# A one-core decode block: head-by-head query projection, a bf16 bias product, and 64 streamed columns in the wo and w1 products

## The chip, the cores and the metric

The kernel runs on one core of a Trainium2 chip. The metric is the device time of one execution in microseconds (us). One execution is also recorded by the hardware profiler; its span, from the first to the last instruction, is about 1.5 us shorter than the time in most runs. Engines are named as in the profile: PE (matrix products), PEld (its weight loads), DVE (vector), ACT (scalar), POOL, and SP, whose sequencer (SPq) issues most transfers.

## The reference, cut to what matters

```python
# x: 4 x 1 x 640 (batch 4, one token); 32 heads of 128; cache of 4096 positions; all bf16
q = (layernorm(x) @ wq)                                   # wq 640 x 4096
scores = einsum("bhqd,bhkd->bhqk", q, k_cache) * 128**-0.5 # k_cache 4 x 32 x 4096 x 128
o = einsum("bhqk,bhkd->bhqd", softmax(scores), v_cache)
h = x + o.reshape(4, 1, 4096) @ wo                        # wo 4096 x 640
g = layernorm(h) @ w1 + b1                                # w1 640 x 1728
out = h + (g * tanh(log(1 + exp(g)))) @ w2                # w2 1728 x 640
```

The two caches are 268 MB, the weights 15 MB. There is one token for each of 4 batch rows, so all the projections are products with 4 columns.

## The kernel before, where the change touches it

The heads go in four groups of 8; a tile is the K or V cache of one batch row and one head group (8.39 MB). K tiles are multiplied by the broadcast query on DVE, folded on PE, and V is multiplied on PE. SP asks for tiles as their buffers come free; a V tile can't replace wq before the query has been made. The start:

```python
# query projection: wq is (128, 5, 4096) in a cache buffer, lnT the normalised x, transposed
for h in range(2):
    for c in range(DC):                       # DC = 5 chunks of the 640 inputs
        for hg in range(NHG):                 # 4 head groups, one per 32 output partitions
            mm(red[hg*32:(hg+1)*32, h, :], lnT[:, c, :], wq[:, c, o:o+512], ...)
# two copies red -> q_all (bf16); then spread each head's query over its partitions
for hg in range(NHG):
    for b in range(N):
        for g in range(G):                    # 4 * 4 * 8 = 128 products, 32 rows, 128 columns
            mm(red[:, (2+hg) % 4, b*128:(b+1)*128], sel[r, b, ...], q_all[r, g*128:(g+1)*128], ...)
```

The tail, after the last cache tile (the `mark` and `need` calls, which are semaphores, are left out):

```python
def wo_mm(k):                                 # head group k: 8 x 5 = 40 products of 4 columns
    for j in range(G):
        for c in range(DC):
            w = wo_sb[:, k, j, :].rearrange("p (m c) -> p c m", c=DC)[:, c, :]   # every 5th column
            mm(y_ps[:, c, :], w, a_t[:, k, j, :], False, done)
# ... o, softmax sums, wo_mm(0..3); y -> DVE -> mean and variance by two fp32 products ...
for c0, c1 in ((0, 2), (2, 4), (4, 5)):       # w1 arrives in three pieces
    if c1 == DC - 1:                          # with the second: bias * std, in fp32
        mm(red[:, 2, 0:56], ident_f[:, :], b1s[...], False, False)
    for j in [FM] + list(range(FM)):          # FM = 13: 14 blocks of outputs
        for c in range(c0, c1):
            w = w1_sb[:, c, 0:FM*P].rearrange("p (f j) -> p j f", j=FM)[:, j, :] # every 13th column
            mm(h1_ps[..., j, :], w, cen[:, c, :], False, done)                  # 4 columns
# then h onto the output's bank (40 small products), the activation on DVE and ACT,
# 56 products with w2 (160 columns, 4 side by side in 32-column strips), copy, store
```

The softmax here doesn't subtract the row's maximum and nothing guards it: scores larger than these inputs give would overflow.

## Time and profile before

The time is 663.18 us (median of 3 runs, 662.7 to 663.21). What matters of the profile, whose span is 661.1 us:

| what | us |
|---|---|
| wq landed / first K tile landed | 15.9 / 36.1 |
| one cache tile, landing to landing | 19.3 |
| last piece of w2 landed | 657.5 |
| end | 661.1 |

Landings are read from the transfer records of the trace, piece by piece. The page's slices come first. The rows are 40 equal slices of the span; PEclk is the granted clock of PE in tenths, DMA the busy share of the transfer engines in tenths.

```profile
...
PEclk9768787968658697958767887888876879797965
DMA  9999999999999999999999999999999999999997
GB/s 390 437 444 440 441 417 420 441 436 442 433 436 416 444 436 432 436 440 420 436 436 436 436 436 440 416 444 433 432 440 436 420 440 432 432 440 440 408 420 293
...
```

The transfer engines are at 9 tenths in every slice but the last. They moved 283.50 MB at a mean 429 GB/s, and from 1.65 us to about 655 the records of transfers show never fewer than 16 in flight. So the bytes and their rate set the time of this kernel; at this rate it can gain only before the first transfer or after the last. The next lines are the timeline of the start (start, duration, engine, line, operation, count, and in brackets the idle time before it and what ended it).

```profile
...
16.02 4.42 PE L708 MATMUL red<-slotC,lnT 128*32 128x512 bf16 x40 [6.80 <-PEq L49]
...
21.22 10.31 PE L708 MATMUL red<-q_all,sel 32*128 32x128 bf16 x128 [0.78 <-PEq L49]
...
31.56 0.33 SPq L250 DMA_DIRECT2D slotC<-in_A_v_cache_dram  x1
31.57 0.59 ACT L375 CAST q_bc<-red 128x512 bf16<-128x512 f32 x1 [2.38 <-PE red L708]
...
36.20 8.76 DVE L515 TENSOR_TENSOR slotA<-slotA,q_bc 128x8192 bf16<-128x8192 bf16 x2 [27.27 <-DMA slotA<-in_A_k_cache_dram]
...
```

Read the last line first: DVE was idle 27.27 us and was released by the landing of the K tile, not by the query, whose last copy to q_bc ends at 32.2. The 128 selecting products are the 10.31 us in the second line.

The chain of waits at the end (start, duration, what):

```profile
...
624.24 22.11 DMA slotB<-in_A_wo_dram
...
646.49 1.75 PE y_ps L708 x40
...
648.49 0.63 PE misc L708 x2
...
649.59 5.33 PE red L708 x72
...
656.76 2.16 PE red L708 x31
...
```

From the landing of a piece of wo at 646.35 on, PE and DVE (and once ACT) work in turn, and the chain shows no wait for a transfer: 40 wo products, 72 records on the w1 bank, the activation, the w2 products. Last, the stretches of 3.41 us in which the clock is granted; the columns after the length are the busy times (and counts) of PE, PEld, DVE, ACT and POOL, then the granted clock, the DMA share and GB/s.

```profile
...
core 0: us, PE busy (x) PEld busy (x) DVE busy (x) ACT busy (x) POOL busy (x), PEclk, DMA share, GB/s
641.49:644.90 3.41, 3.03 (x64) 2.73 (x62) 1.51 (x3) 0.00 (x0) 0.00 (x0) 0.50 0.99 416
644.90:648.31 3.41, 2.78 (x67) 2.63 (x64) 0.05 (x1) 0.00 (x0) 0.00 (x0) 0.50 1.02 425
648.31:651.72 3.41, 3.17 (x34) 3.04 (x34) 1.50 (x11) 1.58 (x2) 0.00 (x0) 0.50 1.01 416
651.72:655.13 3.41, 3.41 (x66) 3.24 (x65) 0.19 (x1) 0.00 (x0) 0.00 (x0) 0.50 1.00 416
655.13:658.54 3.41, 2.31 (x88) 1.99 (x78) 1.35 (x6) 0.25 (x1) 0.00 (x0) 0.50 0.33 123
...
```

PE is busy for 82 to 100% of the first four stretches and still has clock 0.50 throughout.

### The profile page before, as it was taken

The page shows a single profiled execution, that of the slowest core. Times are in us where ns is not written, and L with a number is a line of the kernel's source. Part 1 is how long each engine was busy: PE and PEld are TensorE (multiplying, and loading weights), DVE is VectorE, ACT ScalarE, POOL GpSimd, SP SyncE. Part 2 cuts the span into 40 slices and gives each one's busy share as a digit, 9 for nine tenths or more (in the row PEclk, how much of TensorE's full clock was granted, in tenths as well). Part 3 has the DMA queues.
Part 4 walks back from the last instruction along what each step waited for, and adds up shares of the span by engine and source line. Part 5 has one row for each costly group of instructions (what it writes and reads, how often), then busy time and mean ns, then how long its engine had stood idle before and what let it go on. Part 6 is the DMA issues. An engine that isn't in the chain of part 4 may idle for free. (4 is left out here: it accounts for less than half of the span.)

```text
span 661.1 us, 5195 instructions
## 1 busy us (share of the span) xinstructions
PE 396.9 (60%) x2747; PEld 80.8 (12%) x1787; DVE 406.9 (62%) x252; ACT 41.6 (6%) x158; POOL 2.6 (0%) x14
## 2 busy tenths in 40 slices
PE   0856658568317595738407485838434656765767
PEld 0600000101101010101100010000110001010246
DVE  1077988386048779757218798849306798848612
ACT  0200000000000000000000000000000000000011
POOL 1000000000000000000000000000000000000000
PEclk9768787968658697958767887888876879797965
DMA  9999999999999999999999999999999999999997
GB/s 390 437 444 440 441 417 420 441 436 442 433 436 416 444 436 432 436 440 420 436 436 436 436 436 440 416 444 433 432 440 436 420 440 432 432 440 440 408 420 293
DMA packets 6978, 283.50 MB, mean 429 GB/s; under 512 B 1012, under 2 KB 1208, under 8 KB 2232
## 3 DMA queue, kind: packets, MB, share of 16 engines
q1 hardware_dynamic: 6640, 283.27, 99.2%
q8 instruction: 7, 0.11, 0.1%
q10 hardware_dynamic: 328, 0.09, 0.1%
q14 instruction: 3, 0.02, 0.0%
HBM read 283.35 MB, written 0.01 MB: 429 GB/s over the span
## 5 line engine op out<-in xcount | busy, mean ns | idle before, releaser
L515 DVE TENSOR_TENSOR slotA<-slotA,q_bc 128x8192 bf16<-128x8192 bf16 x32 | 140.6, 4416 | 104.3 <-DMA slotA<-in_A_k_cache_dram 104.3
L515 DVE TENSOR_TENSOR slotB<-slotB,q_bc 128x8192 bf16<-128x8192 bf16 x32 | 140.7, 4418 | 16.7 <-DMA slotB<-in_A_k_cache_dram 16.7
L526 DVE TENSOR_REDUCE s_f<-red 128x64 f32<-128x1024 f32 x64 | 78.0, 1219 | 97.7 <-PE red L718 97.6
L718 PE MATMUL red<-slotA,ident 128*128 128x512 bf16 x480 | 136.4, 447 | 0.0
L718 PE MATMUL red<-slotB,ident 128*128 128x512 bf16 x480 | 127.1, 424 | 0.0
L708 PE MATMUL red<-slotA,ident 128*128 128x512 bf16 x32 | 14.6, 456 | 118.9 <-PEq L49 118.9
L708 PE MATMUL pv<-slotC,e 128*32 128x512 bf16 x768 | 53.4, 439 | 36.9 <-PEq L49 33.9
L708 PE MATMUL red<-slotB,ident 128*128 128x512 bf16 x32 | 14.1, 440 | 87.5 <-PEq L49 87.5
L394 ACT ACTIVATE ex<-s_f 128x64 bf16<-128x64 f32 x64 | 16.4, 256 | 503.1 <-DVE s_f L526 503.1
L540 DVE TENSOR_TENSOR e<-ex,hmask 128x512 bf16<-128x512 bf16 x64 | 39.8, 684 | 0.0
L708 PEld LDWEIGHTS pv<-slotC,e 128*32 128x32 bf16 x768 | 22.7, 108 | 96.2 <-issue 82.9
L708 PEld LDWEIGHTS red<-slotA,ident 128*128 128x128 bf16 x32 | 3.2, 99 | 187.7 <-issue 187.6
L708 PEld LDWEIGHTS red<-slotB,ident 128*128 128x128 bf16 x32 | 3.1, 98 | 170.6 <-issue 170.6
L708 PEld LDWEIGHTS o_ps<-pv_sb,selo 128*32 128x32 f32 x136 | 13.5, 109 | 63.0 <-issue 62.9
L708 PE MATMUL o_ps<-pv_sb,selo 128*32 128x128 f32 x136 | 18.0, 276 | 0.0
L708 PE MATMUL pv<-slotA,e 128*32 128x512 bf16 x256 | 14.6, 380 | 0.4 <-PEq L49 0.4
L404 ACT COPY pv_sb<-pv 128x512 f32<-128x512 f32 x16 | 9.4, 586 | 70.4 <-PE pv L708 70.4
L394 ACT ACTIVATION_READ_ACCUMULATOR ex<-s_f 128x1 f32 x64 | 11.9, 186 | 0.0
L708 PE MATMUL red<-q_all,sel 32*128 32x128 bf16 x128 | 10.3, 273 | 0.8 <-PEq L49 0.8
L708 PEld LDWEIGHTS red<-q_all,sel 32*128 32x128 bf16 x128 | 10.1, 124 | 1.6 <-issue 1.6
L708 PEld LDWEIGHTS pv<-slotA,e 128*32 128x32 bf16 x256 | 7.0, 97 | 23.4 <-issue 17.7
L565 DVE RECIPROCAL rl<-misc 32x1 f32<-32x1 f32 x4 | 0.6, 151 | 14.3 <-PE misc L708 14.3
(96 smaller groups left out, 77.8 us busy)
## 6 DMA issues: line engine op xcount, KB each, us to landing
slotC<-in_A_v_cache_dram SPq DMA_DIRECT2D x2, 4096.0 KB, 40.6
slotC<-in_A_wq_dram SPq DMA_DIRECT2D x1, 5120.0 KB, 15.9
slotB<-in_A_wo_dram SPq DMA_DIRECT2D x3, 1280.0 KB, 17.7
slotB<-in_B_w_dram SPq DMA_DIRECT2D x2, 864.0 KB, 25.0
slotB<-in_A_wo_dram SPq DMA_DIRECT2D x1, 960.0 KB, 22.1
slotA<-in_B_w_dram SPq DMA_DIRECT2D x1, 960.0 KB, 25.2
slotA<-in_B_w_dram SPq DMA_DIRECT2D x1, 640.0 KB, 22.4
slotB<-in_B_w_dram SPq DMA_DIRECT2D x1, 432.0 KB, 26.4
```

What stands on the lines that cost most here:

```text
L394: lambda: a.activation(out=ex[:, sl], in_=s_f[:, sl], func=ACT.Exp, scale=SCALE, accum_out=rs[:, b, s : s + 1],),
L404: lambda: a.copy(out=pv_sb[:, :, :].rearrange("p r d -> p (r d)"), in_=pv[:, :]),
L515: lambda: v.tensor_tensor(out=t, in0=t, in1=q_bc[:, hg, b, :].unsqueeze(1).to_broadcast([P, RS, Dh]), op=ALU.mult,),
L526: lambda: v.tensor_reduce(out=s_f[:, s * RS : (s + 1) * RS], in_=red[:, k : k + 2, :].rearrange("p k (r c) -> p (k r) c", c=CW), axis=AX.X ...
L540: lambda: v.tensor_tensor(out=e[:, sl, :], in0=ex[:, sl].unsqueeze(2).to_broadcast([P, RS, G]), in1=hmask[:, :].unsqueeze(1).to_broadcast( ...
L565: dv.do(lambda: v.reciprocal(out=rl[:, :], in_=l_ps), ("rl", hg), DV)
L708: lambda: nc.tensor.matmul(out_, lhsT=lhsT, rhs=rhs, start=start, stop=stop, skip_group_check=skip),
L718: return t.add_instruction(mybir.InstMatmult(name=nc.get_next_instruction_name(), engine=mybir.EngineType.PE, ins=[t.lower_ap(rhs), t.lowe ...
```

## The change

Three parts, meant to shorten the start and the tail. (1) The projection writes each head's query to its own 4 partitions (lnT is padded so that a shifted slice puts the 4 rows in place), so 4 selecting products of 128 rows and 512 columns replace 128 small ones. (2) The bias product, fp32 before, becomes a high and a low bf16 part, moved ahead of the last w1 piece. (3) The moving operand of the wo and w1 products is the 4 columns repeated 16 times: 64 columns stream, of which 4 are used. The wide products are meant to bring PE's clock up: in the stretches above the 4-column products kept PE busy for 82 to 100% and the clock was 0.50.

```diff
-        for h in range(2):
+        GK = G // CG
+        for r in range(GK):
             for c in range(DC):
-                for hg in range(NHG):
+                for k in range(CG):
+                    g = k * GK + r
                     mm(
-                        red[hg * QD : (hg + 1) * QD, h, :], lnT[:, c, :], wq[:, c, o : o + 512],
+                        red[k * QD : (k + 1) * QD, 0, :], lnT[:, c, QD - N * (g + 1) : 2 * QD - N * (g + 1)],
+                        wq[:, c, :].rearrange("p (h g d) -> p g h d", g=G, d=Dh)[:, g, :, :],
 ... (cut)
+        for b in range(N):
+            mm(
+                red[:, (1 + b) % 4, :], sel[:, b * G : (b + 1) * G, :].rearrange("p g q -> p (g q)"),
+                q_all[:, :], True, True, ("qb", b),
+            )
 ... (cut: wo)
-                    mm(y_ps[:, c, :], w, a_t[:, k, j, :], False, done, "y" if done else None)
+                    mm(
+                        y_w[:, c, :, :], w, a_t[:, k, j, :].unsqueeze(1).to_broadcast([P, WD, N]),
+                        False, done, "y" if done else None,
+                    )
 ... (cut: two 512-column products with zeros open the wider bank of w1)
-            if c1 == DC - 1:
-                pe.need("b1s")
-                mm(
-                    red[:, 2, 0 : FC * N], ident_f[:, :], b1s[:, :, :].rearrange("p j n -> p (j n)"),
-                    False, False,
-                )
+            if c1 == DC:
+                pe.need("b1_lo")
+                for part in (b1_hi, b1_lo):
+                    for j0, j1 in ((0, FC // 2 + 1), (FC // 2 + 1, FC)):
+                        mm(h1_ps[:, j0:j1, :], ident[:, :], part[:, j0:j1, :], False, False)
 ... (cut: w1, as wo)
-                        h1_ps[0 : (P if j < FM else FT), j, :], w, cen[:, c, :], False, done,
+                        h1_w[0 : (P if j < FM else FT), j, :, :], w,
+                        cen[:, c, :].unsqueeze(1).to_broadcast([P, WD, N]), False, done,
```

## The prediction

> **What bounds the kernel now.** Transfers. The profile page moves 283.5 MB at a mean 429 GB/s, DMA busy tenths are 9 in 39 of 40 slices, and a count of packets in flight in the trace is 16 from 1.65 us to about 655 us. Landings come in issue order: wq at 15.9 us, the first K tile at 36.1, then a tile (8.39 MB) each 19.3 us (434 GB/s) to the end; the last w2 piece lands at 657.5. After it only 3.5 us remain. The chain of waits follows a transfer of wo landing at 646.35, then PE and DVE: wo products 1.75 us, mean 1.3, w1 products with bias 5.33 (649.59 to 654.92), activation 1.8, w2 products 2.16, copy 0.33, stores to 661.1. So only the last 15 us can respond.

> **Query projection.** The grouped timeline of the start shows 40 matmuls in 4.42 us, two copies of 0.59, then 128 selecting matmuls in 10.31 us. After: still 40 matmuls of 512 columns, one copy, 4 selecting matmuls of 512 columns (0.43 us each at the low clock, from the 128x32x512 matmuls): about 9 us off PE, q_bc ready near 24 us instead of 32.2. But the first multiply starts at 36.20 on the landing of the first K tile, and V's issue (31.56, would be about 23) only joins a queue that is full and in order. Worth 0.

> **The tail.** Windows of 3.41 us show the granted clock 1.0 or 0.5: 1.0 from 638.1 to 641.5, then 0.5 to the end, although PE is busy. [...] But a wo pair (weight load plus 4-column product) takes 43 ns at clock 1.0 (40 in 1.76 us) and 43 ns at 0.5 (40 in 1.73 us), and a w1 pair 65 to 68 ns: the weight load sets the pace, not the clock. Estimated from 128x512 products (427 ns at 0.5[...]), 64 columns need 53 or 27 ns. In w1 they hide in either state; in wo they hide at 1.0, and cost 40 x 10 ns = 0.4 us per head group at 0.5. I expect wo to stay at 1.0 and w1 to fall to 0.5 somewhere. Two 512-column zero products cost 0.4 to 0.8 us more before the third wo group, nearly hidden before the landing at 646.35.

> **Bias.** Two fp32 products (0.66 us in the w1 stream) become four bf16 ones [...] and no longer hold up the middle piece: 0.3 to 0.4 us gained on the chain. The last w1 pieces land at 651.5 and 652.55, so w1 can't end before about 654.4.

> **Limit.** w2's last piece at 657.5 allows at most 1.1 us of gain; that needs w2 at the full clock (52 products in 1.90 us would halve) or act much earlier.

> **Sum.** 0.3 to 0.4 from the bias, 0 to 0.7 from the clock in w2, minus 0 to 0.5 in wo: 663.18 to about 662.8 us. Range 661.9 to 663.9. Faster by over 2%: 0.005; within 2%: 0.985; slower: 0.01.

> **What would show it.** Landings unchanged, 19.3 us apart; first multiply still near 36.2; last query product near 23; clock 1.0 through the wo stage; wo pairs still 43 ns; w1 stage near 4.9 us; w2 landing near 657.5.

> **What would make it wrong.** Weight loads that don't overlap a 64-column product: wo and w1 pairs grow by 25 to 50 ns, costing 3 to 5 us. Or wo staying at 0.5. Or weight loads of w1 that do speed up at clock 1.0, up to the 1.1 us limit.

The trace of before has 427 ns from start to start of 128x512 products at clock 0.5 and 216 at 1.0; an eighth of these is the 53 or 27 ns for 64 columns. The four bf16 products took 0.29 us in the changed kernel (653.56 to 653.85).

## The result, and the profile after

The changed kernel takes 662.12 us (median of 4 runs, 661.6 to 662.67), the kernel before 663.01 in the same rounds. The ratio is 0.9987, with a 95% interval of 0.997 to 1.0004. A ratio here is the mean time of one kernel's fast runs over that of the other's of the same rounds, so it isn't quite the ratio of the medians. Over the nine fast runs of the two comparisons with the changed kernel the mean is 662.24 us, against 662.96 for the 13 runs of before beside them: about 0.7 us less, or 0.1%.

The page's slices of the changed kernel:

```profile
...
PEclk9768787968659796869677887888876769796867
DMA  9999999999999999999999999999999999999997
GB/s 386 444 440 444 421 409 444 437 440 434 437 424 432 436 436 436 440 432 420 440 432 440 436 440 420 436 436 429 444 440 428 424 432 436 440 440 440 400 423 299
...
```

The transfers are as they were. The timeline of its start:

```profile
...
16.12 4.17 PE L714 MATMUL red<-slotC,lnT 128*32 128x512 bf16 x40 [5.99 <-PEq L49]
...
21.07 1.02 PE L714 MATMUL red<-q_all,sel 128*128 128x512 bf16 x4 [0.78 <-PEq L49]
21.48 2.05 ACT L372 CAST q_bc<-red 128x512 bf16<-128x512 f32 x4 [0.56 <-PE red L714]
22.12 0.33 SPq L253 DMA_DIRECT2D slotC<-in_A_v_cache_dram  x1
...
35.48 8.76 DVE L512 TENSOR_TENSOR slotA<-slotA,q_bc 128x8192 bf16<-128x8192 bf16 x2 [25.89 <-DMA slotA<-in_A_k_cache_dram]
...
```

The selecting products take 1.02 us in place of 10.31, V is asked for at 22.12 in place of 31.56, and DVE still waits for the first K tile. The chain of waits at its end:

```profile
...
639.04 2.23 PE y_ps L714 x40
...
642.29 1.72 PE y_ps L714 x40
...
645.32 3.36 PE y_ps L714 x80
...
648.93 0.41 PE misc L714 x2
...
649.82 5.16 PE red L714 x74
...
656.82 2.16 PE red L714 x56
...
```

The w1 stage takes 5.16 us in place of 5.33, the two fp32 statistics products 0.41 in place of 0.63, and the w2 products 2.16 as before. The clock windows of the same stretches (this execution's own windows begin 0.4 us before the stretches chosen):

```profile
...
641.49:644.90 3.41, 3.36 (x60) 3.11 (x58) 1.75 (x4) 0.00 (x0) 0.00 (x0) 1.00 0.97 409
644.90:648.31 3.41, 3.41 (x79) 3.21 (x78) 0.04 (x1) 0.00 (x0) 0.00 (x0) 1.00 1.03 424
648.31:651.72 3.41, 2.88 (x41) 2.53 (x38) 1.81 (x13) 1.55 (x2) 0.00 (x0) 0.94 1.01 421
651.72:655.13 3.41, 3.41 (x66) 3.16 (x67) 0.13 (x1) 0.03 (x1) 0.00 (x0) 0.50 1.01 420
655.13:658.54 3.41, 2.31 (x91) 1.99 (x82) 1.41 (x6) 0.25 (x1) 0.00 (x0) 0.50 0.42 155
...
```

The clock is at 1.00 through most of wo and the first part of w1, and at 0.50 in w2. So in the profiled execution little came of it: from the last w2 landing (657.81) to the end (661.16) pass 3.35 us, against 3.59 before (657.52 to 661.11). This execution was also the slowest of the four: its span was 661.2 us, the others' 660.1 to 660.8. The experiments had to say what the others did.

### The profile page after: what moved, and what is told of

The parts are those of the page before. It is cut to its first block, busy times and chain, and to the rows that moved or that the text cites. A ratio compares the mean times of both kernels' runs of the same rounds, so it can differ in the third digit from the quotient of the medians.

```text
span 661.2 us, 4952 instructions
## 1 busy us (share of the span) xinstructions
PE 388.1 (59%) x2626; PEld 70.3 (11%) x1666; DVE 407.5 (62%) x254; ACT 40.7 (6%) x157; POOL 1.7 (0%) x12
## 5 line engine op out<-in xcount | busy, mean ns | idle before, releaser
L714 PE MATMUL red<-slotC,lnT 128*32 128x512 bf16 x40 | 4.2, 597 | 6.0 <-PEq L49 6.0
L714 PE MATMUL y_ps<-a_t,slotB 128*128 128x64 bf16 x160 | 7.6, 213 | 0.0
```

The source lines that it names most:

```text
L714: lambda: nc.tensor.matmul(out_, lhsT=lhsT, rhs=rhs, start=start, stop=stop, skip_group_check=skip),
```

## The experiments

The table gathers the last 4 us of every profile that bears on the tail. "w2 clock" is the granted clock in the w2 stage, "w2" the duration of its 56 products.

| run | w2 clock | w2, us | last w2 landing | end | difference |
|---|---|---|---|---|---|
| before | 0.5 | 2.16 | 657.52 | 661.11 | 3.59 |
| before_look | 0.5 | 2.16 | 657.72 | 661.34 | 3.62 |
| q_only | 0.5 | 2.16 | 657.54 | 661.27 | 3.73 |
| bias_only | 0.5 | 2.16 | 657.92 | 661.23 | 3.31 |
| wide_only | 1.0 | 1.27 | 657.87 | 661.08 | 3.21 |
| after | 0.5 | 2.16 | 657.81 | 661.16 | 3.35 |
| after_again | 1.0 | 1.32 | 657.55 | 660.05 | 2.50 |
| after_look | 1.0 | 1.35 | 657.54 | 660.04 | 2.50 |
| w1_wide | 0.5 | 2.17 | 657.72 | 661.98 | 4.26 |
| fill_narrow | 0.5 | 2.16 | 657.61 | 661.23 | 3.62 |
| fill | 1.0 | 1.33 | 657.84 | 660.34 | 2.50 |
| contig | 0.5 | 2.9, waits for the landing | 657.61 | 660.17 | 2.56 |

q_twice and q_late, not in the table, had clock 0.5, 2.16 us and differences of 3.66 and 3.69. So all eight profiles with 4 columns in wo and w1 had the low clock in w2, and four of the six with wide w1 products had the full one.

The difference is worth more than the time here: the landings themselves move by 0.4 us between executions, and the difference leaves that out.

### q_only: the projection alone

Edit: part (1) of the diff on the kernel before, nothing else.

> The kernel before with the query projection of the change alone. Main theory (the gain is made after the last wo landing, the projection has slack until the first K tile lands near 36 us): q_bc ready near 23.5 us in place of 32.2, first multiply still within 0.7 us of 36, ratio to before 1.000 +- 0.0007, tail from the first-part landing of the fourth wo group to the end 14.7 us as before. Rival (the projection is worth part of the gain): 0.3 to 0.9 us faster, landings of the K and V tiles earlier throughout.

Measured: 663.06 us (662.78 to 663.88, 5 runs), ratio 1.0005 (0.9992 to 1.0019). The first three cache tiles landed 0.85 us earlier (the first at 35.25 in place of 36.1), but the fourth at 94.10 (94.00 before) and the last w2 piece at 657.54 (657.52). So the projection, 9 us shorter on PE, gives nothing, as the main theory said.

### bias_only: the bf16 bias alone

Edit: part (2) on the kernel before, with 4 columns throughout.

> The kernel before with the bf16 bias product alone, 4 columns throughout. Main theory: this is where the tail's gain comes from; w1 stage about 4.95 to 5.15 us in place of 5.33 (held to that by the landing of the middle w1 piece), tail 0.2 to 0.4 us shorter, ratio 0.9995. Rival: nothing, tail 14.7 us.

Measured: 662.45 us (662.39 to 662.74), ratio 0.9993 (0.9979 to 1.0006); all five runs but one lie below the lowest of the nine runs of before beside them (662.70). In its chain of waits the w1 stage takes 4.93 us in place of 5.33:

```profile
...
650.11 4.93 PE red L717 x72
...
```

The difference falls to 3.31; the five profiles with the fp32 bias in one piece and strided 4-column products have 3.59 to 3.73. The interval doesn't exclude 1, but time, stage and difference agree: this part is worth 0.3 to 0.5 us.

### wide_only: the 64 columns alone

Edit: part (3) on the kernel before. The wide w1 products write two banks of `red` in place of one, and the fp32 bias is split in two with them.

> The kernel before with the 64-column wo and w1 products alone, bias still in fp32. Main theory (weight loads set the pace, 42 to 43 ns in wo and 59 to 60 ns in w1 in either clock state): no gain, 0 to +0.4 us, because a wo group takes 2.2 us where the clock is 0.5 and 1.7 where it is 1.0. Rival (the clock raised by the wide products makes the tail shorter): tail after the fourth wo landing 0.3 us or more shorter than 14.7 us, time 0.3 to 0.9 us lower.

Measured: 663.26 us (661.81 to 663.72), ratio 1.0001 (0.9987 to 1.0015). On the time the main theory holds, but its reason doesn't. In the profile the w1 stage took 5.91 us (the split fp32 bias cost 1.03 us for four records in place of 0.66 for two), and the clock was back at 1.0 in w2, which took 1.27 us in place of 2.16. A loss and a gain cancelled. From its chain of waits:

```profile
...
649.87 5.91 PE red L711 x74
...
657.62 1.27 PE red L711 x56
...
```

The single runs spread over 1.9 us, where those of before spread over 0.5.

### after_again and after_look: the changed kernel again

Edit: none. after_again has 5 rounds; after_look is a single look of unknown state.

> The changed kernel once more, on the chip of the three parts. Main theory: 0.2 to 0.4 us below before (ratio 0.9994 to 0.9997), about the sum of the parts; the 0.9 us of the first comparison was mostly spread of the transfers from run to run. Rival: 0.9 us below again (ratio 0.9987), interval clear of 1.

> A third profile of the changed kernel. Theory: one of two outcomes, by where the 3.41 us windows fall: w2 at clock 1.0, about 1.35 us, end 2.5 us after the last w2 landing (as in the second profile), or at 0.5, about 2.15 us, end 3.3 us after it (as in the first). Nothing between.

Measured: after_again 662.58 us (661.4 to 662.88), ratio 0.9994 (0.9981 to 1.0008), so the median gain is 0.4 us this time. But its profile, and that of after_look, show what the first profile didn't: w2 at the full clock. The chain of waits of after_look:

```profile
...
646.68 1.77 PE y_ps L714 x40
...
649.59 5.07 PE red L714 x74
...
656.50 1.35 PE red L714 x56
...
```

The w2 products take 1.35 us in place of 2.16, and the end comes 2.50 us after the last landing in place of 3.35. So the tail has two outcomes in the three profiles taken, as expected before after_look. In the clock records of after_again the clock fell to 0.5 at 651.77, one window at 0.5 full of w1 products followed, and at 655.18 it was raised again, in time for w2; after_look shows the same 0.25 us later. In the first profile it fell at 651.33 and stayed at 0.5. Its next window also held w1 products, but in it PE waited about 0.2 us for the second piece of w1 (landed at 651.70; in after_again the same wait, 651.26 to 651.50, fell before the window).

### before_look: the kernel before again

Edit: none.

> A second profile of the kernel before. Theory: in w2 the granted clock is 0.5 whatever the place of the 3.41 us windows[...]; w2 stage 2.1 to 2.2 us, end 3.5 to 3.7 us after the last w2 landing. Rival (the phase decides for both kernels): w2 at 1.0 here, end 2.5 us after that landing.

Measured: 662.85 us, clock 0.5 from 641.84 to the end, w2 2.16 us, difference 3.62. With 4 columns both profiles have the slow w2.

### w1_wide: wo back at 4 columns

Edit, on the changed kernel:

```diff
-                        y_w[:, c, :, :], w, a_t[:, k, j, :].unsqueeze(1).to_broadcast([P, WD, N]),
+                        y_ps[:, c, :], w, a_t[:, k, j, :],
```

> The changed kernel with the wo products back at 4 columns, w1 still at 64. Theory (wide wo gives nothing that the end keeps; wide w1 at the low clock [...]raises the clock for w2 in some executions): wo pairs 43 ns whatever the clock, spread of the spans as in the changed kernel (660.0 to 661.2), ratio 0.9990 to 0.9997. Rival (the wide wo products carry the gain): spans all near 661.2 and the w2 stage always near 2.1 us.

Measured: 662.9 us (661.95 to 664.59), ratio 0.9994 (0.9981 to 1.0008). The spans were 660.2 to 662.0. Two of five runs reached the short end without wide wo products, and the profiled one shows what wide wo is for. There the clock was 0.5 from 629.75 on; the two 512-column products that open the w1 bank took 0.77 us in place of 0.45 (in wide_only, at 1.0), the last two wo groups ended late, and y was copied at 649.24, 2.56 us after the fourth wo landing (646.68); before it was 1.91 (648.26 after 646.35). From its chain of waits:

```profile
...
645.28 0.77 PE red L714 x2
...
```

The window that held the end of the V products and the start of wo had a share (by the count above) of 0.66 here, from 636.58, and of 0.95 in the first profile of the changed kernel, from 637.68, and the clock rose there alone. It rose before the third wo group in all five profiles with wide wo and in five of the nine with 4 columns. So in these profiles an early rise went with wide wo products more often than with 4 columns, which neither theory had; the profiles are few, and the place of the windows differs among them.

### contig: does the weight load set the pace?

Edit, on the kernel before; results are wrong (relative error 0.044), traffic and counts the same:

```diff
-                    w = wo_sb[:, k, j, :].rearrange("p (m c) -> p c m", c=DC)[:, c, :]
+                    w = wo_sb[:, k, j, c * P : (c + 1) * P]
-                        w = w1_sb[:, c, 0 : FM * P].rearrange("p (f j) -> p j f", j=FM)[:, j, :]
+                        w = w1_sb[:, c, j * P : (j + 1) * P]
```

> The kernel before, with the wo and w1 weights of each product taken as 128 adjacent columns in place of every 5th (wo) and every 13th (w1); results wrong on purpose, traffic the same. If the strided weight load sets the pace of a pair: wo pairs fall below 40 ns and w1 pairs well below 59 ns at the same clock, the w1 stage is then held by the landing of its last piece (near 652.5) and ends before 654.2, and the w2 stage either starts before 656 and ends within 0.5 us of the last w2 landing; gain 0.5 to 1.1 us and no more. If the pace is a floor per pair or the clock: pairs unchanged, no gain.

Measured: 661.8 us (661.68 to 662.02), ratio 0.9984 (0.997 to 0.9997). Its timeline, all at clock 0.5:

```profile
...
646.69 1.20 PE L708 MATMUL y_ps<-a_t,slotB 128*128 128x4 bf16 x40 [1.06 <-DMA slotB<-in_A_wo_dram]
...
649.53 1.02 PE L708 MATMUL red<-cen,slotB 128*64 128x4 bf16 x28 [0.33 <-DMA slotB<-in_B_w_dram]
...
655.12 0.30 PE L708 MATMUL red<-w_tail,act 64*4 64x160 bf16 x4 [1.10 <-DVE act L697]
...
655.35 2.61 PE L708 MATMUL red<-slotA,act 128*4 128x160 bf16 x52
...
658.01 0.33 DVE L704 CAST o_bf<-red 128x160 bf16<-128x160 f32 x1 [2.94 <-PE red L708]
...
```

The 40 wo products take 1.20 us, where columns 10 bytes apart took 1.73 in the kernel before; their starts are 27 ns apart in place of 40. The first 28 w1 products take 1.02 us in place of 1.92, with starts 27 ns apart in place of 59 to 60. The clock and the columns are the same, so the stride of the weight load set the pace. The activation was ready at 655.12 in place of 656.76, 1.64 us earlier, but the end came only 0.94 us earlier in these two profiles (1.1 in the medians): the w2 stage, still at the low clock, now waits for its last piece (657.61) and ends 0.4 us after it. That is the limit that the prediction named.

### fill and fill_narrow: holding the clock up

Edit of fill, on the changed kernel: 96 columns in w1, and four products of 512 columns without use where PE waits.

```diff
+        fill(pv)            # an identity product with 512 columns of q_bc into a bank that is free
         pe.need("st")
+        fill(y_full)
         pe.need("cen")
-                        cen[:, c, :].unsqueeze(1).to_broadcast([P, WD, N]), False, done,
+                        cen[:, c, :].unsqueeze(1).to_broadcast([P, 24, N]), False, done,
+        fill(y_full)
+        fill(y_full)
         pe.need("act")
```

The wider w1 bank takes all four banks of `red`, so y2 moved to another. fill_narrow has the same four products on bias_only, with 4 columns everywhere.

> The changed kernel with 96 columns in the w1 products and four 512-column products without use put where PE waits (before the copy of y, before the centred rows, two before the activation). Theory (the w2 products' clock is what varies between executions of the changed kernel: 2.16 us cold, 1.35 us at full clock): the clock stays 1.0 to the end in every execution, w2 stage about 1.3 us, end within 0.5 us of the last w2 landing, spans of all runs 659.9 to 660.4, ratio to before about 0.9985. If the products without use delay the chain or the clock falls anyway: no better than the changed kernel, spans 660 to 661.3.

> The kernel before with the bf16 bias and the four products without use, wo and w1 at 4 columns. If the wide columns are what keeps the clock up: clock 0.5 in w1 and w2, w2 stage about 2.15 us, the products without use take 0.43 us each and delay the chain by 0 to 0.4 us, ratio 0.9990 to 1.0003. If the four products alone are enough: w2 about 1.35 us and 661.8 us, as with the wide columns.

Measured: fill is correct and takes 661.85 us (661.66 to 661.97), ratio 0.9983 (0.9969 to 0.9996), with spans of 660.1 to 660.4; in its trace the clock is 1.0 from 639.16 to 659.64. Four of its windows, and the w2 stage from its timeline:

```profile
...
644.90:648.31 3.41, 3.35 (x78) 3.15 (x77) 0.00 (x0) 0.00 (x0) 0.00 (x0) 1.00 1.04 426
648.31:651.72 3.41, 3.10 (x43) 2.59 (x41) 1.81 (x13) 1.52 (x2) 0.00 (x0) 1.00 1.02 424
651.72:655.13 3.41, 3.41 (x78) 3.16 (x79) 0.12 (x1) 0.06 (x1) 0.00 (x0) 1.00 1.00 410
655.13:658.54 3.41, 2.06 (x94) 1.33 (x80) 1.74 (x7) 0.25 (x1) 0.00 (x0) 1.00 0.37 138
...
```

```profile
...
656.82 0.24 PE L715 MATMUL o_ps<-w_tail,act 64*4 64x160 bf16 x4 [0.77 <-DVE act L704]
...
656.99 1.13 PE L715 MATMUL o_ps<-slotA,act 128*4 128x160 bf16 x52
658.17 0.33 DVE L711 CAST o_bf<-o_ps 128x160 bf16<-128x160 f32 x1 [1.40 <-PE o_ps L715]
...
```

PEclk is 1.00 where the kernel before has 0.50, and 52 of the w2 products take 1.13 us in place of 1.90. All five runs are short, so the spread of the changed kernel goes when the clock is held. fill_narrow takes 662.84 us (662.66 to 662.91), ratio 0.9996 (0.998 to 1.0013): clock 0.5 from 629.55 to the end, w2 2.16 us. Four products without use are not enough: its clock was low before the first of them, and no window of its tail had a share above 0.69. With the wide columns (64 in wo and 96 in w1) the clock rose, and no window counted less than 0.46 until the one in which w2 ended. Whether the wider columns or the four products would do alone was not run.

fill is the fastest correct kernel, by 1.1 us over the kernel before. Its last copy starts 0.33 us after the last w2 landing (657.84, 658.17), so little more is to be had from PE's clock.

### q_twice and q_late: how much slack has the start?

Edit, on the kernel before: all 128 selecting products twice (q_twice), or 64 of them twice (q_late).

```diff
-        for hg in range(NHG):
+        for rep, hg in [(r, h) for r in range(2) for h in range(NHG)]:          # q_twice
+        for rep, hg in [(0, 0), (0, 1)] + [(1, h) for h in range(NHG)]:         # q_late
```

> The kernel before with the 128 selecting products of the query projection done twice, about 10 us more on PE ahead of the first multiply. Main theory (the full in-order transfer queue makes the start worth nothing): first multiply moves from 36.2 to about 42.5 us, the landings of all later tiles and the end don't move, ratio 1.000 +- 0.001. Rival (the start is on the path of the time): 6 to 10 us slower (ratio 1.010 to 1.015).

> The kernel before with 64 of the 128 selecting products done twice, about 5 us more on PE at the start (the doubling of all of them moved the first multiply from 36.2 to 43.7 us and cost 2.3 us at the last K and V landings, with one tile asked for only 2.8 us before its predecessor landed). Theory (the start is free until an issue comes within a few us of the queue running dry): first multiply near 37.5 to 39 us, the fifth issue near 65 us and still 8 us or more ahead of the landing before it, landings 19.3 us apart throughout, ratio 1.000 +- 0.001. Rival (every us of the start beyond the first K tile's landing costs a third of a us): ratio 1.001 or more, last K and V landings 0.5 us later.

Measured: q_twice takes 666.0 us (665.01 to 667.69, 4 runs), ratio 1.0054 (1.0039 to 1.007). Both theories are wrong. The first multiply and the issues of the next tiles, from its timeline:

```profile
...
43.73 8.76 DVE L515 TENSOR_TENSOR slotA<-slotA,q_bc 128x8192 bf16<-128x8192 bf16 x2 [34.64 <-ACT q_bc L375]
...
```

```profile
...
71.42 0.33 SPq L250 DMA_DIRECT2D slotA<-in_A_k_cache_dram  x1
92.47 0.33 SPq L250 DMA_DIRECT2D slotC<-in_A_v_cache_dram  x1
...
```

The multiply starts 7.5 us later, and so do the buffers come free. The V tile was asked for at 92.47, only 2.8 us before the landing ahead of it (95.25); in the kernel before the same issue was 10.3 us ahead (83.67, 94.0). In the records of transfers in flight the engines lost 0.9 us between 90 and 100 us, where the kernel before lost none. The landing of the next K tile is 2.4 us late (135.01, 132.6 before), and from there on the tiles keep their 19.3 us to the end. Counted in bytes moved, this execution falls behind the kernel before by 1.5 us between 92 and 97 us: 0.9 of idle engines, and the rest in transfer records that took longer (2.70 us in the mean in place of 2.42). The issue at 71.42, 3.8 us ahead of its landing, cost 0.2, and one at 130.15, 4.9 us ahead, nothing. Another 0.6 us was lost between 34 and 42 us, when no tile was late; why stays open. The profile is that of the fastest of the four runs (665.01), so the others lost more. q_late moved the first multiply to 38.0; the issue at 85.74 was 8.3 us ahead of the landing before it (94.08), and the closest of the whole run, at 590.85, 5.8 us. It lost nothing: 663.05 us, ratio 1.000 (0.9983 to 1.0017). So the start has slack of at least 1.8 us and less than 7.5. The projection moves the query forward from 32.2 us to 23.5, where the K tile's landing at 35 to 36 already covers it.

## Why the prediction was right

**Time.** 662.8 was predicted, with 661.9 to 663.9 as range; the first comparison gave 662.12, the second 662.58. The range of 2 us holds both outcomes of w2, and no change at all as well, so the total tests little; the terms of the sum are what the experiments tested. Three of the first comparison's four spans are 660.8 or less, and two of the second's five; the kernel is the same, so that the first came out lower may be chance.

**Transfers bound the body.** Right. Tiles land 19.3 us apart in both kernels, and fill, contig and the changed kernel all end between 660.0 and 661.2 us in their profiles.

**Projection worth 0.** Right, shown by q_only. The reasoning behind it, that a full queue makes the start free, is true only as far as q_late: q_twice shows that the slack ends before 7.5 us.

**Bias 0.3 to 0.4 us.** Right: 0.5 us in the medians of bias_only, 0.3 to 0.4 in the difference, 0.40 in the w1 stage. The w1 stage was expected near 4.9 us. It took 4.93 in bias_only, and 5.07 (after_look) and 5.16 (first profile) in the changed kernel: its 64 columns lengthen the last 14 products (1.19 us in after_look, 1.09 in bias_only), and in the first profile PE waited for the second piece.

**Weight loads, not the clock, set the pace of wo and w1.** Right, shown by contig, and by the spacing of the records: w1 products start 59 to 60 ns apart at clock 0.5 with 4 columns and at both clocks with 64. A group of wide wo products takes 2.23 us at 0.5 (for its first 2.05 us) and 1.72 at 1.0, 0.5 us more where 0.4 was expected. "Clock 1.0 through the wo stage" was half right: in the first profile the first group ran at 0.5, because the clock rose at 641.09 there.

**0 to 0.7 us from the clock in w2.** That w2 can get the full clock was right, the size a little low: the limit of 0.7 for this term was too small by 0.1. w2 at the full clock takes 0.81 to 0.84 us less (2.16 to 1.35 or 1.32), and this happened in two of three profiles. The prediction's middle (0.4 us of gain in all) gave it too little weight; the mean gain of nine runs is 0.7.

**At most 1.1 us.** Right. contig and fill, two quite different ways to shorten the tail, both stop there: ratios 0.9984 and 0.9983, and 2.56 and 2.50 us after the last landing.

Where did 9 us of PE work and a doubled clock go? The 9 us lay under the wait for the first K tile. In wo and w1 the clock isn't the pace: 4-column wo products start 40 ns apart at either clock (before), and 64-column w1 products 59 to 60 (after). What is left is 0.3 us of bias and 0.8 us of w2 in the executions in which w2 runs at clock 1.0 (two of three profiles).

## What to carry to other kernels

Ask what a product's pace is before paying for clock. Here, with 4 columns, the weight load was the pace, and its stride mattered where the clock didn't: it took the starts of w1 products from 27 to 59 ns apart at clock 0.5 (contig, before), and at clock 1.0 the 59 stayed as they were (after). Columns streamed for nothing gave w2, the stage that did need it, the full clock in four of the six profiles with wide w1 products (1.27 to 1.35 us in place of 2.16), and in none of the eight with 4 columns. By the count, no window at 0.5 with a share below 0.72 was followed by 1.0, and the share depended on where the windows fell. So look at several executions, and fill PE's waits as well if it has to hold: in fill, with 96 columns in w1 as well, the clock was 1.0 from 639.16 to 659.64. When transfers are never short of work, measure gains from the last landing to the end, and count how far ahead of the landing before it each issue comes before trusting slack at the start: here 4.9 us and more lost nothing, 3.8 us lost 0.2 and 2.8 us lost 1.5 (q_twice, q_late).
